# Tile 0's probabilities scaled on GpSimd, and three empty steps behind tile 0's attention items

## The chip, the core and the metric

The kernel runs on one core of a Trainium2 chip. The core has five engines that matter here: TensorE (PE, matrix products into PSUM; its weight loads are listed as PEld), VectorE (DVE), ScalarE (ACT), GpSimd (POOL), and SyncE (SP), whose queue issues nearly all DMA transfers. The metric is the time of one execution on the device in microseconds (us); lower is better. Three runs of the kernel before gave 931.55, 928.86 and 931.79 us, with a median of 931.55.

## The reference, cut to what matters

Attention over 4 batches of 8 heads, 512 local positions in a window of 32 to both sides plus 32 global positions, head size 64. Then two feed-forward layers over the 2304 tokens that come out, 512 wide:

```python
s_l = concat([scale * q_l @ k_g.T, where(mask, scale * q_l @ k_l.T, -1e9)])   # window 32
out_l = softmax(s_l) @ concat([v_g, v_l])        # softmax divides by (sum + 1e-9)
out_g = softmax(scale * q_g @ k_all.T) @ v_all
x = [out_g, out_l] as 2304 tokens x 512
h = x @ w_in                                     # 512 -> 2048
x = where(h >= 1, h, where(h <= -1, 0, (h + 1)**2 / 4)) @ w_out
y = ((x @ w_a) * (x @ w_b)) @ w_out2             # 512 -> 1536 -> 512
```

## The kernel before, in words

The tokens are cut into 18 blocks of 128 and six tiles of three blocks (`TILES`, the last one two blocks wide). Attention of a tile consists of items: one `Local` item for each of the tile's three blocks and each of four head pairs, so tile 0 is items 0 to 11, tile 1 items 12 to 23. For one item:

- `load` and `load_v` fetch q/k (`qk`, 176 KB) and v on SP's queue.
- `s_pe` (L200) makes the scores of both heads on PE; `fill` (L205) adds `NWARM` matmuls of the identity that nothing reads, for items 3 to 11.
- `s_post` adds the mask, scales and takes the minimum on DVE (L213, one instruction a head, writing the item's tile `e`, of which there are three) and the exponential with its sum on ACT (L217, one a head).
- `norm` adds 1e-9 and inverts the sums on DVE (L221, L222), and scales head 0 on ACT (L223) and head 1 on DVE (L224).
- `t_pe` (L230) transposes on PE, `t_post` (L234) copies the result out on ACT; `v_pe` (L242) and `v_post` (L248) follow once for each group of three items. For tile 0, `x_chunk` (L358, L359) then splits the result into a high and a low part.

`att_atoms` is a generator that lays these steps out in a software pipeline: at step k it issues the scores of item k, `norm` of item k-1, `v_pe` of the group that ends with item k-3, and the transposes of item k-2. Loads run ahead: an item's `qk` is requested up to five steps early (eight for items under 12). The caller takes one atom at a time with `att_step`.

The program starts with a lone attention phase: `while att_step(ends[0])` runs atoms until tile 0's last group is done. Because of the pipeline, the scores of items 12 to 14, the norms of 12 and 13 belong to that phase too. Every eighth atom also converts one weight tile (`W1.step`, L101 to L111). Then the first feed-forward layer starts. It goes in stages; the first stage is six units of tile 0 (`units`: an `h_unit`, PE lines L470 to L472 into `hp`, and two units later an `x_unit` into `acc`). Among the half units of this stage the atoms of tile 1 are handed out at an even rate, worked out as the number of atoms of the items still to do over the number of half units; what is left is drained behind the stage. The second stage is 16 units of tile 1, with atoms of tile 2 beside them, and so on. Behind the last tile comes the second layer (L625 to L693).

The code's text gives the order in which steps are traced; the framework that builds the program decides the final order of each engine's queue, and it lets instructions of later steps go ahead where they are ready.

A class `Gap` exists (an item without a tile, `t = None`, whose loads do nothing); `att_atoms` skips scores, norms and transposes for such an item. No item list uses it.

Of the kernel before, what the change touches and what calls it, by code (L numbers as in the profile page):

```python
# [44 lines left out]


NNAT = 9
NWARM, WARM_ITEMS = 2, 12
NCOLD = 3
FA = 6  # L50
START_ATOMS = 8
# [13 lines left out]
def body(tc, qk, qkd, vw, kg, vg, w1i, w1o, w2a, w2b, w2o, mask, eye, out):  # L65
    nc = tc.nc
# [24 lines left out]
    def w_load(key, src):  # L91
        raw = sp["p"].tile([P, 512, 2], I32, name="wraw", bufs=sp["raw"])
        nc.sync.dma_start(raw, src.bitcast(I32).rearrange("p (f two) -> p f two", two=2))
        wq.append((key, raw))
# [52 lines left out]
    class Local:  # L147
# [72 lines left out]
        def norm(self):  # L220
            nc.vector.tensor_scalar_add(self.sm, self.sm, 1e-9)  # L221
            nc.vector.reciprocal(self.sm, self.sm)  # L222
            nc.scalar.activation(self.e[:, 0], self.e[:, 0], AF.Copy, scale=self.sm[:, 0:1])  # L223
            nc.vector.tensor_scalar_mul(self.e[:, 1], self.e[:, 1], self.sm[:, 1:2])  # L224

# [24 lines left out]
    class Gap:  # L250
        stk = False
        t = None

        def nop(self):
            pass
# [3 lines left out]
    class Glob:  # L259
        last = True  # L260
        stk = True
        t = -1
# [85 lines left out]
    def widths(t):  # L348
        return P * len(TILES[t])
# [13 lines left out]
    items = []  # L363
    ends = {}
    for t, blks in enumerate(TILES):
        for p in range(NPAIR):
            group = [Local(t, j, blk, p) for j, blk in enumerate(blks) if blk != GLOB]
            for it in group:
                it.group = group
                it.last = it is group[-1]  # L370
            items += group
        for b in GSCHED.get(t, []):
            for q in range(2):
                items.append(Glob(b, q))
        ends[t] = len(items)

    def att_atoms():
        n = len(items)
# [62 lines left out]
    def x_split(t, W):  # L441
        for c in range(NC):
            x_chunk(t, c, W)
        return xs[t]
# [84 lines left out]
    def x_pre(s):  # L529
        n = half_cols(s)  # L530
        for c in range(2):
            t1, t2 = t_tile("t1", c, 0), t_tile("t2", c, 1)
            nc.vector.tensor_tensor(t1[:, :n], xr[(1, c)][:, :n], xr[(0, c)][:, :n], ALU.subtract)
            nc.vector.tensor_tensor(t2[:, :n], xr[(1, 2 + c)][:, :n], t1[:, :n], ALU.subtract)
            tt[(1, c)], tt[(2, c)] = t1, t2
# [19 lines left out]
    def ab_load(u):  # L555

        s, f = divmod(u, NF2)
        for i in range(2):
            t = sp["p"].tile([P, 512], I32, name="wt", bufs=sp["wt"])
            nc.sync.dma_start(f32(t), wd[f][i])  # L560
            wt[(u, i)] = f32(t)
# [38 lines left out]
    def raw_to(n):  # L600
        while rawi[0] < min(n, len(ws2)):
            w_load(*ws2[rawi[0]])
            rawi[0] += 1
# [133 lines left out]
    def paced(fn):  # L737

        with tc.issue_after(at["act"]), tc.issue_after(at["dve"]):
            return fn()  # L740

    def h_unit(t, f):
        W = widths(t)
        if t not in xs:
            x_split(t, W)
        if (t, f) == (0, 0):
            x0_store()
        if (t, f) == (0, FA):
            x0_load()
        hi, lo = xs[t]  # L750
        w = wslots[("i", f)]
        hp = ps.tile([P, 512], F32, name="hp", tag="h")
        for c in range(NC):
            s = slice(c * P, (c + 1) * P)
            mm3(hp[:, :W], w[:, 0, s], w[:, 1, s], hi[c][:, :W], lo[c][:, :W], c == 0, c == NC - 1)
        flush()
        r = mp.tile([P, 384], F32, name="r", tag="r", bufs=3)
        m = mp.tile([P, 384], F32, name="m", bufs=2)
        g = mp.tile([P, 2, 384], F32R, name="g", tag="g", bufs=3)
        gh, gl = g[:, 0], g[:, 1]  # L760
        at["act"] = nc.scalar.activation(r[:, :W], hp[:, :W], AF.Relu, bias=half, scale=0.5 / W_UP).ins  # L761
        nc.vector.scalar_tensor_tensor(m[:, :W], hp[:, :W], 1.0 / W_UP, r[:, :W], ALU.mult, ALU.max)  # L762
        at["dve"] = nc.vector.scalar_tensor_tensor(m[:, :W], r[:, :W], 1.0, m[:, :W], ALU.min, ALU.mult).ins  # L763

        def fin():
            nc.scalar.activation(gh[:, :W], m[:, :W], AF.Copy)  # L766
            nc.vector.tensor_tensor(gl[:, :W], m[:, :W], f32(gh[:, :W]), ALU.subtract)
        deferred.append(fin)
        gq[(t, f)] = (gh, gl)
# [39 lines left out]
    for u in range(len(units)):  # L809
        for kind in (0, 1):  # L810
            if kind == 0:
                if u >= len(units):
                    continue
                t, f = units[u]
                si = stage[u]
                if si == 0:
                    while W1.si < min(2 * f + LEAD1, n1):
                        W1.step()
                if si == 1:
                    want = max(n1 + (len(ws1) - n1) * (f + 1) // (NF1 - 3), 2 * f + LEAD1)  # L820
                    while W1.si < min(want, len(ws1)):
                        paced(W1.step)
                if si == 1 and f == NF1 - 3:
                    es_st.close()
                    sp["p"] = es_st.enter_context(tc.tile_pool(name="pc", bufs=1, reuse_waits="tile"))
                    sp["raw"], sp["wt"] = 2, 2
                    for i in range(2):
                        w_load(*ab2[i])
                if u in conv_at:
                    i = conv_at.index(u)  # L830
                    (nm, f2), tf = paced(w_conv)
                    nc.sync.dma_start(wd[f2]["ab".index(nm)], tf)
                    if i + 2 < len(ab2):
                        w_load(*ab2[i + 2])
                if t == len(TILES) - 2 and f == 0:
                    es_st.close()
                    gp["p"] = es_att.enter_context(tc.tile_pool(name="gp", bufs=1, reuse_waits="tile"))
                if goal[si] < nt and (u == 0 or goal[stage[u - 1]] != goal[si]):
                    todo = items[done["n"]:ends[goal[si]]]
                    n_units = sum(goal[i] == goal[si] for i in stage)  # L840
                    n_atoms = sum(2 + it.last for it in todo)
                    rate = n_atoms / (2.0 * (GLOB_END if t == nt - 2 else n_units) - 1)
                    credit = 0.0
                if (t, f) == (nt - 2, GLOB_END):
                    for _ in att:
                        pass
                    es_att.close()
                    sp["p"] = es_st.enter_context(tc.tile_pool(name="st2", bufs=1, reuse_waits="tile"))
                    sp["raw"], sp["wt"] = RAWBUFS, 4
                    x5p = es_st.enter_context(tc.tile_pool(name="x5p", bufs=1, reuse_waits="tile"))  # L850
                    raw_to(RAWBUFS)
                    ab_load(0)
                h_unit(t, f)
                if (t, f) == (nt - 2, GLOB_END + 1):
                    x_split(nt - 1, widths(nt - 1))
                if t == nt - 1:
                    if f == 0:
                        x1_load(0)
                    elif f == 1:
                        ab_sum(0)  # L860
                        ab_load(1)
                    elif f in (2, 3):
                        ab_split(0, 2 * f - 4)
                        ab_split(0, 2 * f - 3)
                    elif f == 4:
                        x_pre(0)
                    if f >= 5 and f < 12:
                        x_op(0, f - 5)
                    elif f == 14:
                        ab_sum(1)  # L870
                        ab_split(1, 0)
                    elif f == 15:
                        for part in range(1, 4):
                            ab_split(1, part)
            else:
                if u < LAG:
                    continue
                tx, fx = units[u - LAG]
                x_unit(tx, fx)
            if goal[si] < nt:  # L880
                credit += rate
                while credit >= 1.0 and done["n"] < ends[goal[si]]:
                    credit -= 1.0
                    att_step(ends[goal[si]])
        if goal[si] < nt and u + 1 < len(units) and goal[stage[u + 1]] != goal[si]:
            while att_step(ends[goal[si]]):
                pass
# [98 lines left out]
```

## Time and profile before

| | |
|---|---|
| median of three runs | 931.55 us |
| the profiled execution: its time, its span | 930.66 us, 928.9 us |
| PE busy | 918.3 us, 99% of the span |
| DVE busy | 678.5 us, 73% |
| ACT busy | 529.5 us, 57% |
| POOL busy | 0.3 us, five instructions |
| DMA | 114.11 MB, mean 123 GB/s |

The page's chain of work that ended last is 86% PE. PE's busy time is not PE at its peak: matmuls are pipelined, their ends are modelled, and two neighbours overlap, so the time that a group of matmuls really takes from the engine is read from the distance of their starts or from the pieces of the chain, not from the mean duration.

### The profile page before, as it was taken

The page shows a single profiled execution, that of the slowest core. Times are in us where ns is not written, and L with a number is a line of the kernel's source. Part 1 is how long each engine was busy: PE and PEld are TensorE (multiplying, and loading weights), DVE is VectorE, ACT ScalarE, POOL GpSimd, SP SyncE. Part 2 cuts the span into 40 slices and gives each one's busy share as a digit, 9 for nine tenths or more (in the row PEclk, how much of TensorE's full clock was granted, in tenths as well). Part 3 has the DMA queues.
Part 4 walks back from the last instruction along what each step waited for, and adds up shares of the span by engine and source line. Part 5 has one row for each costly group of instructions (what it writes and reads, how often), then busy time and mean ns, then how long its engine had stood idle before and what let it go on. Part 6 is the DMA issues. An engine that isn't in the chain of part 4 may idle for free.

```text
span 928.9 us, 16640 instructions
## 1 busy us (share of the span) xinstructions
PE 918.3 (99%) x5996; PEld 843.4 (91%) x5996; DVE 678.5 (73%) x1755; ACT 529.5 (57%) x1272; POOL 0.3 (0%) x5
## 2 busy tenths in 40 slices
PE   9899999999999999999999999999999999999997
PEld 7678999899999999987899999999999999999996
DVE  5899897677777777744469787777986666976763
ACT  7988776466666666634446465554644444654442
POOL 0000000000000000000000000000000000000000
PEclk9999999999999999999999999999999999999999
DMA  7765664765444544335363233321331111231101
GB/s 221 238 218 166 196 201 136 258 201 178 151 131 132 158 135 129 106 106 163 111 216 120 75 114 93 94 64 58 99 117 46 47 46 46 64 108 58 48 10 57
DMA packets 59442, 114.11 MB, mean 123 GB/s; under 512 B 7264, under 2 KB 28512, under 8 KB 59360
## 3 DMA queue, kind: packets, MB, share of 16 engines
q1 hardware_dynamic: 58784, 112.45, 38.6%
q8 instruction: 47, 0.77, 0.3%
q10 hardware_dynamic: 576, 0.60, 0.2%
q14 instruction: 35, 0.29, 0.1%
HBM read 95.46 MB, written 17.56 MB: 122 GB/s over the span
## 4 chain that ended last, share of the span: by engine, by line
PE 86%; DMA 6%; DVE 4%; ACT 3%; issue 1%; ACTq 0%; SPq 0%; DVEq 0%
PE hp L470 6%; PE hp L472 6%; PE acc L470 6%; PE hp L471 6%; PE acc L471 5%; PE acc L472 5%; PE pb L627 5%; PE pb L628 5%; PE pb L625 5%; PE py L692 5%; PE py L693 5%; PE py L691 5%; PE px L625 4%; PE px L628 4%; PE px L627 4%; DMA wraw<-in_w1o_dram 3%
## 5 line engine op out<-in xcount | busy, mean ns | idle before, releaser
L470 PE MATMUL hp<-xh,w 128*128 128x384 f32 (+1 forms) x384 | 130.5, 340 | 2.3 <-DVE mn L213 1.3
L470 PE MATMUL acc<-g,w 128*128 128x384 f32 (+1 forms) x384 | 130.3, 339 | 0.3 <-ACT g L766 0.2
L472 PE MATMUL hp<-xl,w 128*128 128x384 f32 (+1 forms) x384 | 126.3, 329 | 0.3 <-DVE xl L359 0.3
L471 PE MATMUL acc<-g,w 128*128 128x384 f32 (+1 forms) x384 | 126.4, 329 | 0.0
L472 PE MATMUL acc<-g,w 128*128 128x384 f32 (+1 forms) x384 | 126.0, 328 | 0.0
L471 PE MATMUL hp<-xh,w 128*128 128x384 f32 (+1 forms) x384 | 125.3, 326 | 0.0
L762 DVE SCALAR_TENSOR_TENSOR m<-hp,r 128x384 f32<-128x384 f32 (+1 forms) x96 | 51.2, 533 | 70.8 <-ACT r L761 70.5
L110 ACT ACTIVATE w<-wt 128x512 fp32r<-128x512 f32 (+1 forms) x116 | 65.0, 562 | 64.1 <-PE pb L628 46.6
L627 PE MATMUL pb<-w 128*128 128x384 f32 (+1 forms) x288 | 94.7, 329 | 0.0
L628 PE MATMUL pb<-w 128*128 128x384 f32 (+1 forms) x288 | 94.3, 327 | 0.0
L625 PE MATMUL pb<-w 128*128 128x384 f32 (+1 forms) x288 | 93.7, 325 | 0.0
L761 ACT ACTIVATE r<-hp,half 128x384 f32<-128x384 f32 (+1 forms) x96 | 53.2, 554 | 56.8 <-PE hp L472 56.6
L692 PE MATMUL py<-w,g 128*128 128x512 f32 x204 | 80.7, 396 | 0.0
L693 PE MATMUL py<-w,g 128*128 128x512 f32 x204 | 80.7, 396 | 0.0
L470 PEld LDWEIGHTS hp<-xh,w 128*128 128x128 f32 x384 | 72.4, 189 | 8.6 <-issue 3.3
L691 PE MATMUL py<-w,g 128*128 128x512 f32 x204 | 79.6, 390 | 0.0
L111 DVE TENSOR_TENSOR w<-wsum,w 128x256 fp32r<-128x256 f32 (+1 forms) x108 | 54.7, 508 | 32.1 <-ACT w L110 32.1
L470 PEld LDWEIGHTS acc<-g,w 128*128 128x128 f32 x384 | 72.4, 189 | 5.3 <-issue 3.6
L766 ACT ACTIVATE g<-m 128x384 fp32r<-128x384 f32 (+1 forms) x96 | 48.5, 505 | 47.9 <-DVE m L763 45.7
L472 PEld LDWEIGHTS hp<-xl,w 128*128 128x128 f32 x384 | 72.3, 188 | 2.1 <-DVE xl L359 1.0
L471 PEld LDWEIGHTS acc<-g,w 128*128 128x128 f32 x384 | 72.5, 189 | 0.9 <-issue 0.7
L472 PEld LDWEIGHTS acc<-g,w 128*128 128x128 f32 x384 | 72.4, 188 | 0.5 <-issue 0.5
(113 smaller groups left out, 2055.4 us busy)
## 6 DMA issues: line engine op xcount, KB each, us to landing
wt<-wd SPq DMA_DIRECT2D x72, 256.0 KB, 2.7
qkd<-in_qkd_dram SPq DMA_DIRECT2D x28, 352.0 KB, 3.2
wraw<-in_w1i_dram SPq DMA_DIRECT2D x16, 512.0 KB, 4.1
wraw<-in_w1o_dram SPq DMA_DIRECT2D x16, 512.0 KB, 3.7
v<-in_vw_dram SPq DMA_DIRECT2D x64, 112.0 KB, 3.1
wraw<-in_w2a_dram SPq DMA_DIRECT2D x12, 512.0 KB, 4.0
wraw<-in_w2b_dram SPq DMA_DIRECT2D x12, 512.0 KB, 3.8
wd<-wt SPq DMA_DIRECT2D x24, 256.0 KB, 2.3
```

The lines of the kernel that those rows point to most:

```text
L110: nc.scalar.activation(hi, src, AF.Copy)
L111: nc.vector.tensor_tensor(lo, src, f32(hi), ALU.subtract)
L470: nc.tensor.matmul(acc, whi, xhi, start=first, stop=False)
L471: nc.tensor.matmul(acc, wlo, xhi, start=False, stop=False)
L472: nc.tensor.matmul(acc, whi, xlo, start=False, stop=last)
L625: nc.tensor.matmul(out[:, :n], w[:, 0, r], hi[:, c, :n], start=start and c == 0, stop=False, skip_group_check=True)
L627: nc.tensor.matmul(out[:, :n], w[:, 1, r], hi[:, c, :n], start=False, stop=False, skip_group_check=True)
L628: nc.tensor.matmul(out[:, :n], w[:, 0, r], lo[:, c, :n], start=False, stop=k in (1, 5, 6) and c == 1, skip_group_check=True)
L691: nc.tensor.matmul(a, gh[:, c], w[:, 0], start=f == 0, stop=False)
L692: nc.tensor.matmul(a, gh[:, c], w[:, 1], start=False, stop=False)
L693: nc.tensor.matmul(a, gl[:, c], w[:, 0], start=False, stop=f == NF2 - 1)
L761: at["act"] = nc.scalar.activation(r[:, :W], hp[:, :W], AF.Relu, bias=half, scale=0.5 / W_UP).ins
```

## The change

Tile 0's `norm` sends both heads' scaling to GpSimd in place of ACT and DVE. Three `Gap` items stand behind item 11 in the list, so that at the three steps behind tile 0 no scores are issued; tile 1's items become 15 to 26. `NWARM` goes from 2 to 1. The count of atoms leaves the gaps out (28, as before).

```diff
-NWARM, WARM_ITEMS = 2, 12
+NWARM, WARM_ITEMS = 1, 12
+NGAP = 3
...
         def norm(self):
             nc.vector.tensor_scalar_add(self.sm, self.sm, 1e-9)
             nc.vector.reciprocal(self.sm, self.sm)
+            if self.t == 0:
+                for h in range(2):
+                    nc.gpsimd.tensor_scalar_mul(self.e[:, h], self.e[:, h], self.sm[:, h:h + 1])
+                return
             nc.scalar.activation(self.e[:, 0], self.e[:, 0], AF.Copy, scale=self.sm[:, 0:1])
             nc.vector.tensor_scalar_mul(self.e[:, 1], self.e[:, 1], self.sm[:, 1:2])
...
     class Gap:
         stk = False
         t = None
+        last = False
...
         ends[t] = len(items)
+        if t == 0:
+            items += [Gap() for _ in range(NGAP)]
...
-                    n_atoms = sum(2 + it.last for it in todo)
+                    n_atoms = sum(2 + it.last for it in todo if it.t is not None)
```

## Rows read from the trace of the kernel before

**Rows 1.** The page, part 1: busy time, share of the span, instructions.

```profile
PE 918.3 (99%) x5996; PEld 843.4 (91%) x5996; DVE 678.5 (73%) x1755; ACT 529.5 (57%) x1272; POOL 0.3 (0%) x5
```

**Rows 2.** The page, part 2: TensorE's granted clock in 40 slices, in tenths.

```profile
PEclk9999999999999999999999999999999999999999
```

**Rows 3.** Busy time by stretch: stretch, length, busy of each engine, clock, DMA share, GB/s.

```profile
8.90:42.35 33.45, 32.05 (x253) 24.35 (x253) 26.18 (x115) 31.09 (x95) 0.00 (x0) 1.00 0.72 225
42.35:82.40 40.05, 38.54 (x276) 30.40 (x274) 37.63 (x122) 36.14 (x95) 0.00 (x0) 1.00 0.64 203
82.40:140.00 57.60, 56.75 (x352) 52.68 (x349) 51.39 (x126) 42.13 (x93) 0.00 (x0) 1.00 0.60 190
```

**Rows 4.** Groups by line, PE, 8.9 to 42.35: count, busy, mean ns, idle before.

```profile
L230 PE MATMUL tp<-ident,e 128*112 128x128 f32 x52 | 9.5, 296 | 0.0
L200 PE MATMUL s<-qk 64*128 64x224 f32 x45 | 9.1, 403 | 0.1
L242 PE MATMUL o<-pt,v 112*64 112x128 f32 x96 | 7.0, 281 | 0.0
L205 PE MATMUL warm<-ident 128*128 128x128 f32 x36 | 6.2, 297 | 0.0
```

**Rows 5.** The chain that ended last, pieces: start, us, what.

```profile
1.17 3.96 DMA qk<-in_qk_dram
...
13.15 0.58 PE tp L230 x4
13.73 0.45 PE warm L205 x4
14.18 1.02 PE o L242 x16
...
18.16 0.58 PE s L200 x4
...
41.12 0.36 PE hp L472 x2
```

**Rows 6.** Groups by line, ACT and DVE, 8.9 to 42.35.

```profile
L217 ACT ACTIVATE e<-e,mn 128x224 f32<-128x224 f32 x28 | 13.1, 472 | 0.0
L223 ACT ACTIVATE e<-e,sm 128x224 f32<-128x224 f32 x13 | 6.1, 470 | 0.0
L224 DVE TENSOR_SCALAR e<-e,sm 128x224 f32<-128x224 f32 x15 | 5.0, 335 | 0.3
L103 DVE SCALAR_TENSOR_TENSOR wt<-wraw,wt 128x512 int32<-128x512 int32 x4 | 2.7, 685 | 0.0
L359 DVE TENSOR_TENSOR xl<-xraw,xh 128x384 fp32r<-128x384 f32 x4 | 2.2, 554 | 0.0
L111 DVE TENSOR_TENSOR w<-wt,w 128x512 fp32r<-128x512 f32 x3 | 2.0, 682 | 0.0
```

**Rows 7.** ACT in order of time within one item: start, us, instruction.

```profile
12.48 0.48 ACT L217 ACTIVATE e<-e,mn 128x224 f32<-128x224 f32 x1
...
13.43 0.47 ACT L223 ACTIVATE e<-e,sm 128x224 f32<-128x224 f32 x1
13.80 0.58 ACT L234 ACTIVATE pt<-tp 112x512 f32<-112x512 f32 x1
```

**Rows 8.** DVE in order of time within one item.

```profile
21.35 0.39 DVE L213 CUSTOM_DVE_ANT_0 e<-s,masks 128x224 f32<-128x224 f32 x1 [0.17 <-PE tp L230]
...
21.98 0.17 DVE L221 TENSOR_SCALAR sm<-sm 128x2 f32<-128x2 f32 x1
...
22.38 0.34 DVE L224 TENSOR_SCALAR e<-e,sm 128x224 f32<-128x224 f32 x1
```

**Rows 9.** Who waited for whom, 8.9 to 42.35: total us, times, longest.

```profile
PE hp L470 <- DVE mn L213: 1.3, 2, 0.8
```

**Rows 10.** SP's queue in order of time: a store of the first unit.

```profile
17.45 0.35 SPq L451 DMA_DIRECT2D x0d<-xh  x1
```

**Rows 11.** POOL's last instruction and ACT's table load, in order of time.

```profile
0.73 0.10 POOL L78 MEMSET half<- 128x1 f32 x1 [0.29 <-POOLq L975]
...
2.62 1.28 ACT L217 ACT_TABLE_LOAD   x1 [2.62 <-issue]
```

## The prediction

> **What bounds the kernel now.** I read the engine totals first: PE is busy for 99% of the span and POOL for nothing [rows 1], which seems to leave no room. But PE's busy time counts overlapping and stretched matmuls, so I cut the start of the program into stretches and read busy time by engine [rows 3]. Three stretches matter. From 8.9 to 42.35 us lies tile 0's lone attention, with the first two feed-forward units of 12 `hp` matmuls at its end; from 42.35 to 82.4 the rest of the first stage, with tile 1's attention beside it; from 82.4 on the second stage. In the first stretch ACT is busy 31.09 of 33.45 us, 93%, and DVE 26.18. In the second DVE has 37.63 of 40.05, 94%, and ACT 36.14. In the third DVE has 89% and ACT 73%.
>
> How much PE really needs comes from counts [rows 4] times the pieces of the chain [rows 5], where four transposes take 0.58 us, four score matmuls 0.58, four fillers 0.45, sixteen value matmuls 1.02 and an `hp` matmul 0.18. First stretch: 52/4 x 0.58 = 7.5, 45/4 x 0.58 = 6.5, 96/16 x 1.02 = 6.1, 36/4 x 0.45 = 4.05, 24 x 0.18 = 4.3; together 28.5 of 33.45 us. So PE loses some 5 us there under an engine (ACT) that is fuller than itself, and 4 us are fillers that nothing reads. From 82.4 on PE is nearly dense and the saving of an earlier start would be carried to the end unchanged: nothing behind that point is touched.
>
> **The change part by part.** Sums are made on the profiled execution, 930.66 us (span 928.9 and 1.76 around it); the median of the runs shown is 0.89 above it, and I add the differences to the median.
>
> *Scaling leaves ACT and DVE.* On ACT a scaling occupies the queue from 13.43 to 13.80, 0.37 us [rows 7]; 13 of them lie in the first stretch [rows 6], 11 of tile 0 and two of items 12 and 13, which the gaps move out. ACT loses 13 x 0.37 = 4.8 us. DVE loses some 12 x 0.335 = 4.0 [rows 6].
>
> *Three gaps.* The scores of items 12 to 14 leave the first stretch: on ACT two exponentials each, 12.48 to 13.43, 3 x 0.95 = 2.85 [rows 7]; on DVE two reductions, 21.35 to 21.98, 3 x 0.63 = 1.9, and two norms of 0.40 for add and reciprocal [rows 8] and 0.335 for the scaling, 1.5; on PE 3 x 0.58 = 1.7. They also free the PSUM buffers for which two `hp` groups waited 1.3 us in all [rows 9]; that is part of the 5 us that PE loses, and is not counted twice. SP has three fewer `qk` loads and two fewer v loads in the stretch, and the loads of tile 1 are requested as many steps ahead as before, though three of these steps are now short.
>
> *Fillers.* Nine fills lose half of 0.45 us each: 2.0 us of PE.
>
> First stretch after: PE 28.5 - 1.7 - 2.0 = 24.8; ACT 31.09 - 4.8 - 2.85 = 23.4; DVE 26.18 - 4.0 - 1.9 - 1.5 = 18.8. PE becomes the fullest. If it is as full as the fullest engine is now (93%), the stretch takes 24.8 / 0.93 = 26.7 us, 6.75 less. The ends are 24.8 (PE without a gap, 8.65 less) and 30 (below).
>
> *POOL's price.* The trace has no POOL instruction on more than one column (0.10 us for one [rows 11]). The nearest rows are the same scaling on DVE, 0.335, and on ACT, 0.47; as the far end I take the longest elementwise row of the stretch, 0.685 for 512 columns [rows 6]. I take 0.47, the same shape on an engine that does one thing at a time. Then POOL works 24 x 0.47 = 11.3 us of 26.7, at the far end 16.4, and is not the bound. It lies in the loop through the three `e` tiles: between the reductions of item k and of k+3 lie two steps, some 4.2 us at the new pace, and in them stand the next item's reductions 0.63, add and reciprocal 0.40, two scalings 0.94 and the transposes 0.58, together 2.55. So it is hidden up to about 1.1 us an instruction (24 x 1.1 = 26.4). No other work is queued behind it on POOL.
>
> *What comes back.* The moved scores and norms are now done in the second stretch: PE +1.7, DVE 1.9 + 1.5 = 3.4, ACT 2.85 + 0.75 = 3.6. There DVE is at 94%. If DVE stays so full, the stretch takes (37.63 + 3.4) / 0.94 = 43.6, 3.6 more; if only PE's work counts, since the last atoms can run beside the third stretch where DVE has 6 us free, 1.7 more. I take the middle, 2.6.
>
> Sum: -6.75 + 2.6 = -4.15 us, so 926.5 on the profiled execution and 931.55 - 4.15 = 927.4 as the time.
>
> **The rivals.**
> 1. *The first stretch is held by something else, and the gain is nearly given back.* In it DMA engines are 72% busy at 225 GB/s [rows 3], 7.5 MB; 0.75 MB leave. At the old rate the remaining 6.8 MB take 30 us, a gain of 3.4, less 2.6: 930.8. For it: a `qk` load takes 3.96 us to land even at the start [rows 5], SP's queue is in order, and the framework doesn't keep the text's order: a store that the first unit issues stands at 17.45 in the lone phase [rows 10], so that scores of tile 1 could also be drawn back into it, and the change would not do what it says. Against it: ACT's and DVE's idle time there is put down to other engines. In the same class falls a second stretch that takes the full 3.6 and more.
> 2. *POOL and DVE block each other.* Eleven DVE instructions of the stretch with two inputs in SBUF (L103, L111, L359) take 6.9 us [rows 6]. If each waits for a POOL scaling of 0.47, DVE grows by 5.2, and the chain through `w` and `xl` that ACT and PE wait for by a good part of it; with half of it on the path the stretch takes 29.3 and the time is 930.0. No run here has POOL beside DVE, so rows speak neither for nor against. [...]
> 3. *POOL sets the pace; slower than before.* The place is the lone phase: at 24 scalings, POOL takes longer than the time saved from 30.85 / 24 = 1.29 us an instruction (33.45 less the 2.6 that come back). At 1.5 us the stretch is 36 us: 931.55 + 2.55 + 2.6 = 936.7. For it speaks only that the trace has no price; against it, that it needs 2.7 times ACT's row.
> 4. *A one-time load before POOL's first scaling.* The first transposes start at 8.9 us and, with three `e` tiles, the whole phase stands until they are through. ACT's own one-time load took 1.28 us [rows 11], a transfer from memory 3.96 [rows 5]: 927.4 + 1.3 to 4 gives 928.7 to 931.4. The trace shows none on POOL, whose only instructions are memsets. [...]
> 5. *Fewer fillers and the clock.* The granted clock is full in every slice [rows 2]. Were the lower of its two levels granted through the new first stretch, PE's 24.8 us would double and the time be near 950. Against it: PE is fuller than before even without the fillers (24.8 of 26.7, before 28.5 of 33.45).
>
> **How the numbers follow.** The forecast, 925.5 to 928.7, gets 0.47. That it goes better, a denser first stretch and the second giving back only 1.7 or less (down to 922.8), gets 0.13: PE's bound alone would give 931.55 - 8.65 + 1.7 = 924.6. Rival 1 gets 0.17, rival 2 0.09, rival 3 0.07, rival 4 0.05 (of which 0.01 slower), rival 5 0.02. About 0.3% (2.8 us) is what a measurement of this kernel can tell from no change: faster is below 928.75, slower above 934.35. So faster 0.47 + 0.13 = 0.60, the same 0.17 + 0.09 + 0.04 = 0.30, slower 0.07 + 0.01 + 0.02 = 0.10. The range reaches from 922.8 to 932.0, over rivals 1, 2 and most of 4, and leaves out rivals 3 and 5.
>
> **What would show it.** Right: the last of the second unit's `hp` matmuls ends near 35.6 us in place of 42.35; ACT is below 90% busy up to there; 24 POOL instructions of 0.34 to 0.69 us, the transposes not waiting for them; the granted clock full; the first stage ends near 78 us, and from there the two traces run in parallel to the end. Wrong: POOL busy above 90% in the lone phase, or PE's and DVE's waits ending on POOL (rivals 2 and 3); a first POOL instruction that starts late (rival 4); ACT and DVE idle before DMA (rival 1); scores of tile 1 on PE before tile 0's last value matmuls; the second stretch longer than 46 us, which gives the gain back.

## The result: 0.96% slower, where 0.4% faster was forecast

The changed kernel takes 939.53 us (median of 7 runs, 936.17 to 944.26), the kernel before 930.82 in runs beside it; the ratio is 1.0096, with a 95% interval of 1.0078 to 1.0114. The forecast was 927.4, with a range of 922.8 to 932.0. The profiled execution took 940.68 us.

The page's second part, the granted clock in 40 slices, against [rows 2]:

```profile
PEclk7899999999999999999999999999999999999999
```

The first two slices are short of full speed. Busy time by stretch (stretch, length, busy of PE, PEld, DVE, ACT and POOL with the number of instructions, granted clock, DMA share, GB/s), first the three stretches of [rows 3], then finer ones:

```profile
8.90:42.35 33.45, 30.25 (x166) 20.14 (x166) 16.96 (x71) 20.23 (x56) 19.18 (x22) 0.69 0.53 165
42.35:82.40 40.05, 37.71 (x252) 29.04 (x253) 33.98 (x114) 33.44 (x87) 0.93 (x2) 1.00 0.66 211
82.40:140.00 57.60, 57.39 (x385) 51.37 (x384) 51.16 (x143) 44.68 (x107) 0.00 (x0) 1.00 0.58 185
...
10.80:20.00 9.20, 9.19 (x44) 6.31 (x46) 2.41 (x14) 4.25 (x13) 4.97 (x6) 0.51 0.34 96
20.00:31.00 11.00, 11.00 (x56) 7.65 (x54) 5.73 (x24) 6.67 (x19) 5.16 (x6) 0.50 0.42 132
31.00:45.60 14.60, 11.67 (x93) 7.64 (x93) 8.31 (x31) 9.93 (x25) 8.12 (x9) 0.98 0.68 211
```

In the first stretch ACT is busy 20.23 of 33.45 us and DVE 16.96: both were relieved as planned, and neither is near full. But from 10.8 to 31 us the granted clock is 0.50 to 0.51, and PE, busy all the time there, works at about half speed: four transposes take 1.10 us at 30.11 and 0.60 at 32.19.

Four marks on the way show where the time goes (start, us, instruction): tile 0's last value matmuls; the last `hp` matmul of the second unit, which ends the prediction's first stretch; the first `hp` matmul of the second stage, which ends its second stretch; and the second stage's first store of `part` (duration in ns min/median/max, then first and last start in us). Before:

```profile
37.53 0.66 PE L242 MATMUL o<-pt,v 112*64 112x128 f32 x8
42.17 0.34 PE L472 MATMUL hp<-xl,w 128*128 128x384 f32 x1
82.46 0.44 PE L470 MATMUL hp<-xh,w 128*128 128x384 f32 x1
L791 SPq DMA_DIRECT2D part<-x x4: 327/364/531, 91.8 to 93.3; - x4
```

After:

```profile
43.70 1.53 PE L247 MATMUL o<-pt,v 112*64 112x128 f32 x24
50.55 0.34 PE L480 MATMUL hp<-xl,w 128*128 128x384 f32 x1
93.97 0.44 PE L478 MATMUL hp<-xh,w 128*128 128x384 f32 x1
L799 SPq DMA_DIRECT2D part<-x x4: 344/389/413, 102.0 to 103.4; - x4
```

Tile 0's last value matmuls end at 45.2 us, in the kernel before at 38.2. The first stretch ends 8.4 us later (50.55 against 42.17). The second stretch, from there to the next mark, takes 43.4 us against 40.3. At the first store the changed kernel is 10.2 us behind, and from then on the two traces run in parallel, 10 us apart, to the end.

What PE and POOL did around the fall of the clock can be read in the order of time (start, us, instruction; in brackets the idle time before it and what ended that):

```profile
7.45 3.31 POOL L226 TENSOR_SCALAR e<-e,sm 128x224 f32<-128x224 f32 x4 [6.63 <-DVE sm L222]
...
8.34 0.43 PE L235 MATMUL tp<-ident,e 128*112 128x128 f32 x2 [0.66 <-POOL e L226]
9.17 0.43 PE L235 MATMUL tp<-ident,e 128*112 128x128 f32 x2 [0.39 <-POOL e L226]
9.32 0.30 PEld L206 LDWEIGHTS warm<-ident 128*128 128x128 f32 x2
...
9.99 0.43 PE L235 MATMUL tp<-ident,e 128*112 128x128 f32 x2 [0.17 <-POOL e L226]
10.81 0.54 PE L235 MATMUL tp<-ident,e 128*112 128x128 f32 x2 [0.39 <-POOL e L226]
...
10.97 0.51 PEld L206 LDWEIGHTS warm<-ident 128*128 128x128 f32 x2
...
37.56 5.72 POOL L226 TENSOR_SCALAR e<-e,sm 128x224 f32<-128x224 f32 x6 [1.30 <-PE o L247]
```

The first four scalings stand back to back on POOL, 0.83 us each. Every pair of transposes waits for one of them; then, in the middle of the fourth pair, the weight load of a filler goes from 0.15 to 0.25 us. At the end of the phase six scalings stand back to back, 0.95 us each in the mean. The groups and the waits of the stretch (8.9 to 45.6 us; count, busy, mean ns, idle before; then total us, times, longest):

```profile
L235 PE MATMUL tp<-ident,e 128*112 128x128 f32 x46 | 11.1, 356 | 3.9 <-POOL e L226 3.9
...
L112 DVE TENSOR_TENSOR w<-wt,w 128x512 fp32r<-128x512 f32 x3 | 2.2, 740 | 0.0
...
L104 DVE SCALAR_TENSOR_TENSOR wt<-wraw,wt 128x512 int32<-128x512 int32 x3 | 2.1, 685 | 0.0
```

```profile
DVE e L214 <- PE tp L235: 8.4, 5, 2.2
ACT pt L239 <- PE tp L235: 8.2, 8, 2.2
...
PE tp L235 <- POOL e L226: 3.9, 9, 0.7
```

PE waits 3.9 us for POOL, and DVE and ACT wait 8 us each for a slow PE. POOL's own row for the whole program (count, busy, mean ns, idle before), and its shortest, median and longest scaling in ns:

```profile
L226 POOL TENSOR_SCALAR e<-e,sm 128x224 f32<-128x224 f32 x24 | 21.6, 914 | 20.9 <-DVE sm L222 9.4 <-PE warm L206 5.2 <-ACT w L111 2.9
...
L226 POOL TENSOR_SCALAR e<-e,sm x24: 840/845/1349, 7.4 to 42.4; 128x224 f32<-128x224 f32 x24
```

### The profile page after: what moved, and what is told of

It reads as the page before. It is cut to its first block, busy times and chain, and to the rows that moved or that the text cites. A ratio compares the mean times of both kernels' runs of the same rounds, so it can differ in the third digit from the quotient of the medians.

```text
span 938.9 us, 16609 instructions
## 1 busy us (share of the span) xinstructions
PE 924.8 (98%) x5978; PEld 844.4 (90%) x5978; DVE 674.3 (72%) x1743; ACT 526.5 (56%) x1260; POOL 21.8 (2%) x29
## 4 chain that ended last, share of the span: by engine, by line
PE 86%; DVE 5%; DMA 4%; ACT 3%; POOL 1%; issue 1%; POOLq 0%; ACTq 0%; DVEq 0%; SPq 0%
PE hp L478 6%; PE acc L478 6%; PE hp L480 6%; PE hp L479 6%; PE acc L479 6%; PE acc L480 6%; PE pb L635 5%; PE pb L636 5%; PE pb L633 5%; PE py L700 5%; PE py L701 5%; PE py L699 5%; PE px L635 4%; PE px L633 4%; PE px L636 4%; PE tp L235 2%
## 5 line engine op out<-in xcount | busy, mean ns | idle before, releaser
L111 ACT ACTIVATE w<-wt 128x512 fp32r<-128x512 f32 (+1 forms) x116 | 65.3, 563 | 66.2 <-PE pb L636 46.6
L112 DVE TENSOR_TENSOR w<-wsum,w 128x256 fp32r<-128x256 f32 (+1 forms) x108 | 54.7, 508 | 32.1 <-ACT w L111 32.1
```

Source lines behind the costliest of these rows:

```text
L111: nc.scalar.activation(hi, src, AF.Copy)
L112: nc.vector.tensor_tensor(lo, src, f32(hi), ALU.subtract)
```

## The experiments

Two theories. The clock theory: holes on PE (times in which it waits for another engine) let the granted clock fall, and PE's work at half speed is the loss. The pace theory: POOL's scaling is so long that it sets the pace of tile 0, whatever the clock. The rivals were the fillers and the gaps by themselves. In the table, "clock" is the mean over a kernel's executions of each one's granted clock averaged over its span; 0.001 less is 0.93 us of PE time lost in a span of 930 us, if PE is what counts. The kernel before has 0.9993 over 34 executions beside e1 to e4, and 0.9989 to 0.9993 beside e5 to e13. Each ratio is to the kernel before as it ran beside that kernel, with medians of 929.8 to 930.8 us. e6, e9, e10 and e13 have four executions each, e12 has five, the others seven to twelve.

| kernel | GpSimd | gaps | fillers | median us | ratio, 95% interval | clock |
|---|---|---|---|---|---|---|
| e4 | - | - | 1 | 929.6 | 0.9992 [0.9983, 1.0002] | 0.9992 |
| e3 | - | 3 | 2 | 930.7 | 1.0000 [0.9990, 1.0011] | 0.9989 |
| e2 | both heads | - | 2 | 930.5 | 1.0006 [0.9993, 1.0018] | 0.9987 |
| e1 | - | 3 | 1 | 933.6 | 1.0030 [1.0014, 1.0046] | 0.9965 |
| e5 | both heads | 3 | 2 | 934.3 | 1.0047 [1.0032, 1.0062] | 0.9965 |
| e9 | both heads | - | 1 | 937.7 | 1.0078 [1.0059, 1.0098] | 0.9940 |
| after | both heads | 3 | 1 | 939.5 | 1.0096 [1.0078, 1.0114] | 0.9943 |
| e10 (after again) | both heads | 3 | 1 | 939.3 | 1.0090 [1.0066, 1.0115] | 0.9930 |
| e6 | from item 3 | 3 | 1 | 938.6 | 1.0092 [1.0065, 1.0119] | 0.9935 |
| e8 | both heads | 3 | 1, and 8 three times | 934.1 | 1.0034 [1.0019, 1.0050] | 0.9970 |
| e13 | both heads | 3 | 4 | 935.7 | 1.0054 [1.0038, 1.0069] | 0.9938 |
| e7 | one head | 3 | 1 | 932.2 | 1.0026 [1.0011, 1.0041] | 0.9967 |
| e11 | one head | - | 2 | 930.2 | 0.9997 [0.9983, 1.0011] | 0.9975 |
| e12 | one head | - | 2, tile 1: 1 | 934.1 | 1.0039 [1.0027, 1.0052] | 0.9984 |

**One part alone.** e4, on the kernel before:

```diff
-NWARM, WARM_ITEMS = 2, 12
+NWARM, WARM_ITEMS = 1, 12
```

> The kernel before with one filler matmul in place of two for items 3 to 11, nothing else. If ACT bounds the stretch, PE's 2.0 us are hidden and the time is 929.5 to 931 with the clock at 1.00 (clock and pace theories). If the fillers are what holds the clock, it falls below 0.9 in some stretch between 9 and 34 us and the time is 934 or more.

929.6 us, the clock full (0.9992), as the first forecast had it. e3, on the changed kernel, so that only the gaps are left:

```diff
-            if self.t == 0:
-                for h in range(2):
-                    nc.gpsimd.tensor_scalar_mul(self.e[:, h], self.e[:, h], self.sm[:, h:h + 1])
-                return
-NWARM, WARM_ITEMS = 1, 12
+NWARM, WARM_ITEMS = 2, 12
```

> The kernel before with only the three gaps. By the sum of the prediction without POOL: ACT 31.09 less 2.85 and 0.75 in the first stretch is 27.5, at 93% 29.6 us, 3.9 less; the second stretch 1.7 to 3.6 more: 929 to 931 (before 930.8). Rival, the gaps cost: the first stretch keeps its length because loads or the order of the queues hold it, and the second grows: 933 to 935. Clock 1.00 by all theories.

930.7 us. In its trace tile 0's last value matmuls end at 35.2 us, 3.0 earlier (3.9 were expected), and `part` is first stored at 89.7 instead of 91.8, so 0.9 of it is given back; the rest, 2.1, is seen in the trace (its span is 926.8 against 928.9 us) and not in the medians. e2, on the kernel before:

```diff
+            if self.t == 0:
+                for h in range(2):
+                    nc.gpsimd.tensor_scalar_mul(self.e[:, h], self.e[:, h], self.sm[:, h:h + 1])
+                return
             nc.scalar.activation(self.e[:, 0], self.e[:, 0], AF.Copy, scale=self.sm[:, 0:1])
```

> The kernel before with only tile 0's scaling moved to GpSimd (two fillers, no gaps). Clock theory: PE waits for POOL at 8 to 11 us as in the changed kernel, the clock falls to about 0.5 for some 20 us, time 937 to 943. Pace theory: POOL's 24 x 0.9 = 21.6 us is less than the 33 us that ACT needs in this stretch of the kernel before, so the pace hardly changes: 930 to 934, clock at 1.00. Fillers theory (one filler is what lets the clock fall): clock at 1.00 and 928 to 933.

930.5 us: no loss, but no gain either from taking 4.4 us off ACT. Of its 12 executions 11 had a mean clock of 0.998 or more and took 929.4 to 931.6; the profiled one had 0.992 and took 935.45. In it the clock falls in the same place as in the changed kernel:

```profile
8.20:10.80 2.60, 1.73 (x11) 1.12 (x12) 1.08 (x6) 1.22 (x4) 2.49 (x4) 1.00 1.02 358
10.80:20.00 9.20, 9.20 (x44) 6.43 (x45) 2.30 (x14) 4.21 (x13) 4.98 (x6) 0.50 0.38 96
20.00:25.00 5.00, 5.00 (x22) 3.29 (x22) 2.94 (x11) 3.82 (x9) 1.66 (x2) 0.55 0.41 129
```

So with two fillers and tile 1's scores beside it the kernel mostly keeps the clock, and pays 5 us where it doesn't. The clock theory's 937 to 943 was a miss for the median, and too high even for the one execution that lost the clock; the pace theory's 930 to 934 held, and so did the fillers theory's 928 to 933.

**Two parts.** e1 is the changed kernel with the four lines on GpSimd taken out.

> The changed kernel with tile 0's scaling back on ACT and VectorE (three gaps and one filler stay). Clock theory (POOL's slow first scalings open holes on PE at 8.3 to 10.8 us, the granted clock falls to half until 31, and that is the loss): the holes go, the clock stays at 1.00, time 927 to 931, near the kernel before or a little under. Pace theory (POOL's 0.83 to 0.95 us a scaling in the loop of the three e tiles is the loss, whatever the clock): also 927 to 931. Rival, the fillers: with one filler the clock falls even without POOL, 0.5 to 0.6 in 10 to 30 us, and the time is 936 or more. Rival, the gaps: clock at 1.00, but the second stretch takes 6 us or more than before and the time is over 933.

933.6 us, without any work on POOL. The clock is full through the lone phase (1.00 in every stretch to 45 us) and falls later, at some 61 us (its stretches, in the columns of before):

```profile
55.00:60.00 5.00, 3.75 (x22) 2.93 (x22) 2.57 (x7) 2.46 (x8) 0.00 (x0) 1.00 0.70 207
60.00:65.00 5.00, 4.79 (x14) 3.09 (x15) 5.00 (x20) 4.67 (x14) 0.00 (x0) 0.58 0.44 138
65.00:70.00 5.00, 5.00 (x25) 4.96 (x24) 1.66 (x7) 1.91 (x6) 0.00 (x0) 0.73 0.41 138
```

Ahead of the fall PE is busy 3.75 of 5 us: ACT waits 2.5 us for a weight tile from memory, and DVE for ACT. Its 11 executions follow the clock: 929.0 us at 1.000, 931.6 to 932.3 at 0.997 to 0.998, 933.6 to 934.7 at 0.996, 935.3 and 936.6 at 0.994. Both main theories missed here. The gaps rival had the time right, over 933, but wanted the clock at 1.00, and the fillers rival wanted the fall at 10 to 30 us and 936 or more; neither had this place.

e5 is the changed kernel with two fillers (`NWARM` 2).

> The changed kernel with two fillers again (GpSimd and gaps stay). Measured so far: GpSimd alone 930.5, gaps alone 930.7, one filler alone 929.6, all three 939.5, gaps and one filler 933.6. Pair theory A, GpSimd and the gaps clash (without tile 1's scores beside them the last items of tile 0 stand in POOL's queue with nothing else to do): 935 to 940 here too. Theory B, the clash is one filler with POOL (the clock is lost for good only with one filler): 929 to 932. Clock theory as the whole loss: runs with a mean clock of 0.999 or more lie at 928 to 931, and the time goes with the clock alone.

934.3 us. In the trace the clock holds through the start (1.00 to 31 us) and falls at the end of the lone phase, where PE stands for POOL's last scalings:

```profile
31.00:37.00 6.00, 3.95 (x35) 2.26 (x33) 2.81 (x7) 3.49 (x9) 4.33 (x4) 0.95 0.84 251
37.00:45.00 8.00, 8.00 (x43) 6.14 (x44) 5.23 (x15) 4.24 (x13) 0.00 (x0) 0.82 0.63 193
```

PE waits 4.5 us for POOL in this trace. Theory A's range is just missed, theory B is out. The two executions at a clock of 0.999 and 1.000 took 932.0 and 934.2, over the 928 to 931 that the clock theory gave them, so in these two the recorded clock is not the whole loss. e9 is e2 with one filler (`NWARM` 1).

> The kernel before with GpSimd and one filler, without the gaps. Measured: GpSimd and gaps 934.3, gaps and one filler 933.6, GpSimd alone 930.5. If the gaps are what makes the other two dear (they take away the work that PE had while it waited): 930 to 932, mean clock 0.998 or more in most runs. If POOL with one filler is dear by itself: 934 or more, clock 0.995 or less. By the clock theory the time is 930 plus 0.93 us for each 0.001 that the mean clock is short of 1.

937.7 us, without any gaps, clock 0.991 to 0.997:

```profile
20.00:25.00 5.00, 3.44 (x20) 2.21 (x20) 2.80 (x15) 3.01 (x10) 2.38 (x3) 0.75 0.54 180
25.00:31.00 6.00, 6.00 (x34) 4.44 (x32) 2.92 (x10) 2.91 (x8) 3.10 (x4) 0.50 0.43 138
```

The second forecast, 934 or more, held. So it isn't one pair that clashes. No part alone shows a cost (the intervals of e2 to e4 reach to 1.0018 at most, 1.7 us); each pair does, and in each the clock is lower. The gaps are not what makes the pairs dear.

**The changed kernel again**, unchanged.

> The changed kernel once more, for a second trace and more pairs of time and mean clock (so far 936.2 and 936.4 at 0.999, 939.5 to 944.3 at 0.988 to 0.994). Clock theory with a blind start (the recorded clock shows 1.00 until the first change of level, while the weight loads of PE run at half speed, 0.245 against 0.133 us a filler): slow executions at a recorded 0.999 have half-speed loads well past 10 us. Pace theory: in such an execution loads are at full speed and PE waits for POOL 5 us or more longer than the kernel before lost.

939.3 us; the four executions had clocks of 0.991 to 0.997, so the long execution at a recorded 0.999 did not come again, and that question stays open. The trace shows the same holes at 8 to 17 us, but the clock holds over them (1.00 to 20 us) and falls at some 22 us, in a wait of 0.98 us for POOL (0.72 from 20 to 25 us, 0.50 from 25 to 31). So the holes go ahead of the fall, but the same holes do not bring it every time.

**Where the clock is lost.** e6 takes the first three items off GpSimd:

```diff
+            self.n = 3 * p + j
...
-            if self.t == 0:
+            if self.t == 0 and self.n >= 3:
```

> The changed kernel with items 0 to 2 of tile 0 scaled on ACT and VectorE, GpSimd from item 3 on (18 scalings in place of 24). Clock theory: PE's holes at 8.3 to 10.8 us go, the clock is kept in the first 20 us, and the time falls from 939.5 by most of the loss, to 928 to 933. Pace theory: clock or not, tile 0's last items still queue on POOL (six scalings of 0.95 us back to back at the end), so 934 to 937.

938.6 us. The clock holds to 36 us (1.00 to 31), as expected, and is lost at the other end for 14 us, behind a stretch in which PE is busy 3.76 of 6 us:

```profile
31.00:37.00 6.00, 3.76 (x36) 2.46 (x35) 5.14 (x16) 4.70 (x11) 5.36 (x5) 0.97 0.62 171
37.00:45.00 8.00, 7.56 (x38) 5.14 (x38) 1.63 (x5) 2.15 (x5) 1.06 (x2) 0.50 0.32 114
```

Both ranges were missed: with the first place cured, the fall comes at the next. e8 puts fillers where the first holes are:

```diff
                 it = items[k - 2]
+                if k - 2 < NCOLD:
+                    for _ in range(8):
+                        it.fill()
                 it.t_pe()
```

> The changed kernel with eight filler matmuls ahead of each of the first three transposes, some 1.8 us of PE work each, in the place where PE waits for POOL. Clock theory: the clock stays at 1.00 through 8 to 31 us and the time is 928 to 932. Pace theory: the clock is kept but the time is still 934 to 937, since tile 0's last items wait for POOL. If the clock falls all the same (mean 0.99), 938 to 942 and nothing is told apart.

934.1 us, 5 us less than the changed kernel with 24 fillers more. The clock holds through the whole lone phase in the trace:

```profile
8.20:10.80 2.60, 2.21 (x17) 1.40 (x15) 0.00 (x0) 0.95 (x3) 2.60 (x4) 1.00 1.05 373
10.80:31.00 20.20, 18.78 (x155) 13.69 (x155) 16.61 (x64) 17.13 (x48) 15.17 (x15) 1.00 0.71 227
31.00:45.00 14.00, 12.67 (x102) 9.48 (x104) 10.44 (x38) 10.62 (x30) 5.67 (x6) 1.00 0.78 242
```

and yet two of the marks come later than in the kernel before:

```profile
38.07 1.53 PE L247 MATMUL o<-pt,v 112*64 112x128 f32 x24
44.47 0.34 PE L483 MATMUL hp<-xl,w 128*128 128x384 f32 x1
...
L802 SPq DMA_DIRECT2D part<-x x4: 319/356/412, 92.4 to 94.4; - x4
```

Tile 0's last value matmuls end at 39.6 us (38.2 before), the first stretch ends 2.3 us later than before, where the changed kernel's ended 8.4 later, and the first store is 0.6 us late, where the changed kernel's was 10.2. The trace loses its clock only past 160 us, far from the change (0.85 from 160 to 170 us, where PE is idle for 1.07). The median lies in the pace theory's range, 934 to 937; of the four executions at 0.999, 930.2 to 932.8, two lie in the clock theory's. With the clock kept, the change is worth nothing, and costs little. e13 sets `NWARM` to 4.

> The changed kernel with four fillers for items 3 to 11 (it has one; with two it took 934.3). Clock theory: the clock is kept, mean 0.998 or more in most runs, and though PE has 6 us more work than with one filler the time falls to 930 to 933. Pace theory: fillers only cost, 939 or more. If POOL's pace and the clock each take a part, the time at full clock is 931 to 933 and never under the kernel before.

935.7 us in four executions, less than with one filler and not told apart from two (934.3); none of the three forecasts held. In the profiled execution, the longest of the four, the clock holds as far as the fillers reach (item 11's scores at 31 us) and falls right behind, where the last items wait for POOL with no fillers beside them:

```profile
25.00:31.00 6.00, 6.00 (x49) 4.47 (x50) 5.84 (x20) 5.22 (x15) 2.05 (x3) 1.00 0.82 275
31.00:37.00 6.00, 4.22 (x42) 3.18 (x42) 5.15 (x18) 5.18 (x15) 5.52 (x6) 0.97 0.85 251
37.00:45.00 8.00, 7.70 (x38) 5.51 (x37) 4.04 (x7) 3.53 (x7) 0.66 (x1) 0.50 0.54 184
```

**Half the work on POOL.** e7 leaves head 1 on DVE, in the changed kernel:

```diff
-                for h in range(2):
-                    nc.gpsimd.tensor_scalar_mul(self.e[:, h], self.e[:, h], self.sm[:, h:h + 1])
+                nc.gpsimd.tensor_scalar_mul(self.e[:, 0], self.e[:, 0], self.sm[:, 0:1])
+                nc.vector.tensor_scalar_mul(self.e[:, 1], self.e[:, 1], self.sm[:, 1:2])
```

> The changed kernel with one head's scaling on GpSimd (in ACT's place) and the other back on VectorE. POOL's time for an item falls from 1.7 to 0.83 us. Pace theory: POOL (12 x 0.85 = 10 us) no longer sets the pace and the time is 928 to 932, and PE's waits for POOL go from 7.9 us to under 2. Clock theory: the first item's wait on POOL is halved, the holes on PE at 8 to 11 us shrink to less than 0.5 us each, clock kept mostly: 929 to 934. If the gaps with one filler are the loss: 933 to 935, as without GpSimd.

932.2 us: 7 less than the changed kernel, in the clock theory's range and just outside the pace theory's; 930.3 to 930.7 where the clock was 0.999 or more. PE's transposes wait 2.4 us for POOL in its trace from 8.9 us on, 3.9 in the changed kernel's; the pace theory expected under 2. e11 is the kernel before with only this edit.

> The kernel before with only head 0's scaling of tile 0 on GpSimd instead of ACT (two fillers, no gaps, head 1 stays on VectorE). Pace theory: POOL needs 0.83 us an item, ACT loses 12 x 0.37 = 4.4 us and the clock holds: 927 to 929.5, the best of all. Clock theory: PE's first wait for POOL is short, clock at 0.998 or more: 928 to 930. If the latency of POOL's scaling, twice that of ACT's, takes back what ACT saves: 930 to 931.5.

930.2 us, no faster in the median. But the two executions at a clock of 1.000 took 926.8 and 927.4, the two at 0.999 took 928.1 and 929.0, and the others, at 0.995 to 0.998, 928.5 to 933.0. In the trace the lone phase keeps its clock and tile 0's last value matmuls end at 36.9 us, 1.3 earlier; the clock goes later, behind a thin stretch:

```profile
10.80:37.00 26.20, 23.72 (x205) 16.79 (x206) 21.88 (x95) 21.74 (x67) 9.34 (x10) 1.00 0.72 221
65.00:70.00 5.00, 3.81 (x22) 2.77 (x22) 4.21 (x13) 4.19 (x10) 0.00 (x0) 1.00 0.68 230
70.00:75.00 5.00, 5.00 (x16) 3.90 (x16) 4.21 (x20) 4.59 (x15) 0.00 (x0) 0.58 0.33 90
```

So half of the change, at full clock, hints at the gain that the forecast looked for on ACT: the two executions at 1.000 lie some 2.5 us under the kernel before, which took 929.0 to 930.7 at 1.000 beside them. Two executions don't show it, and the median is in the third forecast's range, where the longer scaling takes back what ACT saves. e12 tries to hold it with a filler for tile 1's items too (e11's edit stays, and `fill` takes a count):

```diff
-                if NCOLD <= k < WARM_ITEMS:
-                    it.fill()
+                if NCOLD <= k < 2 * WARM_ITEMS:
+                    it.fill(NWARM if k < WARM_ITEMS else 1)
```

> One head on GpSimd on top of the kernel before (two fillers, no gaps; 930.2, but 926.8 and 927.4 in the two runs at full clock), and one filler also for the twelve items of tile 1, 2.7 us of PE work, because that kernel's clock fell at 70 to 78 us behind a wait for weights. Clock theory: mean clock 0.999 and more, and if the fillers fall into PE's waits 927 to 929, faster than both kernels; if they stand on PE's path, 929 to 931. If the clock falls as often as without them: 930 to 932.

934.1 us, a miss by every theory: three of five executions had 0.999 or more and still took 931.9 to 934.1, so these fillers cost time with the clock kept, which speaks for their standing on PE's path; the trace loses the clock at 46 us all the same (0.66 from 45 to 50). No kernel tried is faster than the kernel before beyond its interval; the nearest is e4.

## Why the prediction was wrong, by its own steps

The term that failed is the first stretch. The sum had it 6.75 us shorter; by the prediction's own mark it is 8.4 us longer. Two steps were wrong in it: POOL's scaling was put at nothing on the path, and the clock was taken as full. PE waited for POOL, and ran at half speed from 11 to 31 us.

**Right.** PE fullest and ACT and DVE relieved: ACT fell from 31.09 to 20.23 us of busy time in the first stretch, DVE from 26.18 to 16.96. The return in the second stretch: 2.6 us were forecast between 1.7 and 3.6, and the traces show 43.4 - 40.3 = 3.1 by the first `hp` matmul of the second stage, 10.2 - 8.4 = 1.8 by its first store. Nothing changes behind that. No one-time load on POOL (rival 4): its first scaling starts 0.2 us behind the reciprocal that it waits for, and takes 0.83 like the next three, so nothing in the trace stands behind the 0.01 that the forecast counted as slower for it. Rival 2 came in another form. DVE hardly grew: beside POOL, L104 (L103 before) takes 685 ns, as before, and L112 (L111 before) 740 against 682 [rows 6]. POOL did: its longest scaling, 1.35 us against a median of 0.845, starts at 24.1 us together with an L112 on DVE.

**Wrong: POOL's price.** 0.47 us was taken, 0.685 was the far end; it is 0.83 by itself and 0.914 in the mean, 2.5 to 2.7 times DVE's row for the same shape. The bounds came from engines, not from POOL, and their upper end was no bound.

**Wrong: "hidden up to about 1.1 us an instruction".** At 0.91 it was not hidden. The loop through the three `e` tiles counts durations as if items followed each other evenly. They don't, least of all at the two ends: the first two items have nobody ahead of them, so four scalings in a row stand directly ahead of the first transposes, and at the end the last three items put six in a row on POOL, 5.72 us, while DVE and ACT are half idle (3.96 and 4.74 us busy from 37 to 45). That the gaps make this end, by taking tile 1's scores away, is argued and not shown. The working also leaves out the exponentials, 0.95 us an item [rows 7], which stand between an item's reductions and its reciprocal. PE waits 3.9 us for POOL. With the clock held by fillers (e8) the first stretch ends at 44.8 us and not near 35.6.

**Wrong: the argument against rival 5.** It was that PE would be fuller, 24.8 of 26.7 us, so the clock would hold with fewer fillers. The 26.7 rested on POOL being hidden. With the waits PE is thinner, and each of the three parts makes it so: one filler less in each of nine items, three items' scores less, and waits for POOL. The table shows that one part is borne and two are not: one filler less, without the rest, keeps the clock (e4, 929.6). Rival 5 had 0.02 of the chances, at 950 for the whole stretch; it came for 20 of the 33 us in the profiled execution.

**The sizes.** The mean clock of the changed kernel is 0.0050 under that of the kernel before, 4.7 us at 0.93 us for 0.001; the slope among its own executions (0.57 us for 0.001) would make it 2.9. So of the 8.7 us between the medians some 3 to 5 are the clock by this count. The profiled executions give it more. Length times the missing share of the clock, from the rows above, is 9.2 x 0.49 + 11.0 x 0.50 + 14.6 x 0.02 = 10.3 us of PE time, and the changed kernel is 10.2 us behind at the first store. The same sum up to that store, against how far it is behind, gives 6.8 and 8.9 for e10, 6.8 and 10.3 for e6, 6.8 and 8.1 for e9, 1.7 and 4.2 for e5, 0 and 0.6 for e8. In e2 it is 6.8 and only 4.6, so the sum is a bound on what the clock cost and not the cost itself. In the traces, then, the clock can be most of the loss. What the rest is made of is not settled: two executions of the changed kernel at a recorded 0.999 took 936.2 and 936.4, e8 with the same POOL work and the same gaps took 930.2 to 932.8 at that clock, and no trace of the former exists.

## What to carry to other kernels

An engine that has no row of the kind in the trace has no upper bound from other engines' rows (0.83 us here, over the 0.685 taken as the far end): measure its instruction first, and look at the two ends of a pipeline, where a longer latency has nothing to hide under. Work that nothing reads, or that stands beside a wait by accident, can hold TensorE's clock (in e8, with 24 fillers more, it is 1.00 from 10.8 to 31 us, where the changed kernel's is 0.50; in e2, with tile 1's scores left in place, its mean is 0.9987, in e5 without them 0.9965); before taking it away, or making PE wait, look for PE's thinnest stretches all along the path, because with one cured the clock may fall at the next (0.50 from 37 to 45 us in e6 and e13). And when a kernel's times scatter, set each against that execution's own mean clock: the two executions of e11 at 1.000 hint at a gain that its median hides.

## What the runs showed of the hardware that was not expected

The clock is not a matter of a kernel alone: the same program kept it in 11 executions of 12 (e2), and another lost it at 11 us in one execution and at 22 in the next (after, e10). And the recorded clock doesn't always see the start. In the profiled execution of the kernel before, the row says 1.00 throughout, yet the weight loads of four fillers take 0.97 us at 9.57 and 0.53 two us later:

```profile
9.57 0.97 PEld L205 LDWEIGHTS warm<-ident 128*128 128x128 f32 x4
...
11.63 0.53 PEld L205 LDWEIGHTS warm<-ident 128*128 128x128 f32 x4
```

That is 0.24 and then 0.13 us a load. 0.25 us is what the changed kernel shows where the recorded clock falls to half (0.51 for two at 10.97), so PE ran at half speed to some 10 us there without a record. In this trace the length of a weight load (0.24 against 0.13 us, under one recorded clock of 1.00) is the better gauge.
